# Two transposes swapped on a queue: k of batch b+1 ahead of C's exponentials of batch b, and the next loads placed behind q's transpose

## The chip, the cores and the metric

One core of one Trainium2 chip runs the whole kernel. The metric is the device time of one execution in microseconds (us); less is better. On one core, "slow" marks a run over 1.5% above the fastest of its kernel. Medians and ranges are over all executions, slow ones included. Ratios are the mean time of one kernel's fast runs over that of the other's fast runs of the same rounds, so they are not quite the ratio of the medians quoted beside them.

## The reference

Nystrom attention with 8 batches, 8 heads, 576 positions and 32 landmarks, followed by a gated feed-forward layer:

```python
q_lm = q.reshape(B, H, m, S // m, D).mean(axis=3)      # landmarks, k_lm likewise
A, Bm, C = sm(q, k_lm), sm(q_lm, k_lm), sm(q_lm, k)    # softmaxes
Z = Bm^T / (norms of Bm);  6 times: Z = 2 Z - Z @ Bm @ Z
x = A @ Z @ C @ v                                      # attention
out = (sigmoid(x @ w_gate) * (x @ w_val)) @ w_out
```

## The kernel before

The program is woven from streams (front, mid, value, norm, newton, ffn1, ffn2). A planning clock inside the kernel (`model`) guesses when each engine is free and when each tile has landed, and emits TensorE's instructions in the order of these guesses. On the chip that order is fixed: TensorE takes its instructions in turn, whatever is ready.

Names that the profiles use: klm and bq are the landmarks of k and q as TensorE takes them; bs, sl and sa are the scores of Bm, C and A; cl holds C's exponentials, ct the same transposed, cv is C @ v. Bc is Bm, Bt the same transposed; bdT and bd are Bt and Bc spread over the diagonal blocks of a larger matrix; s and sy belong to the iteration for Z. an is A. U and V are the rest of x times w_gate and w_val. gp and vp are the gate and value products of the feed-forward layer, th and ht what ScalarE and VectorE make of them, op the last product and ob its copy out of PSUM, where the kernel's matmuls leave their results. A transfer "lands" when its data has arrived.

The front of a late batch turns k and q by crossbar transposes issued on SP, sums them on GpSimd (POOL) to landmarks, and swaps halves by DMA:

```python
for what in ("k", "q") if b >= TURN else ():
    ...
    turned[what] = turn(t, ..., n, ...)                 # nc.sync.dma_start_transpose
for what in ("k", "q"):
    ...
    pool.tensor_add(out=s1, in0=t[:, :, 0:P6], in1=t[:, :, P6:2 * P6])    # 128 x 768
    pool.tensor_add(out=s2, in0=s1, in1=t[:, :, 2 * P6:3 * P6])           # 128 x 768
    if b >= SWAP and what == "k" and b < B - 1:
        load(b + 1, "k")
        load(b + 1, "q")
    ...                                                 # s3, s4: 128 x 256
# swaps of s4's halves by DMA on SP, then klm, bq on POOL, then load(b + 1, "v")
def fronts():
    for b in range(B):
        ...
        if b > TURN:
            yield made(turned_c, b - 1)                 # ct of b - 1 is issued
        yield from front(b)
```

The middle of a batch, on VectorE (DVE) between matmuls:

```python
turn(ct, ct, cl, ...)                                   # ct: C's exponentials, transposed
spread(bdT, Bt)          # two tensor_mul, blk x Bt, bf16, 128 x 128
...
dve.tensor_reduce(out=ce, in_=n1, axis=AX.X, op=ALU.max)            # n1 in PSUM (this is cc)
dve.tensor_scalar_add(out=ce, in0=cc, scalar1=1e-6)                 # 128 x 2, fp32
dve.reciprocal(out=rc, in_=ce)
...                      # S0 scaled by rc
spread(bd, Bc)           # two tensor_mul, blk x Bc, bf16, 128 x 128
```

The softmax here doesn't subtract the row's maximum and nothing guards it: scores larger than these inputs give would overflow.

Of the kernel before, what the change touches and what calls it, by code (L numbers as in the profile page):

```python
# [177 lines left out]
def kernel(ctx, tc, q, k, v, moe_w_gate, moe_w_val, moe_w_out, out):  # L178
# [14 lines left out]
    B, H, S, D = q.shape  # L193
# [20 lines left out]
    TURN, LATE = 3, 2  # L214
    PLAIN = min(TURN, LATE)

    SWAP = 3
# [14 lines left out]
    def bank(shape, dtype, name, hold=False):  # L232

        return model.take(ps.tile(shape, dtype, name=name, tag="p", bufs=BANKS), hold)

    def done_with(*tiles):
        model.held -= {t.name for t in tiles}

    def mm(slow=0.0, **kw):
        rhs, lhsT = kw["rhs"], kw["lhsT"]  # L240
        n = 1
        for x in rhs.shape[1:]:
            n *= x
        c = 1
        for x in lhsT.shape[1:]:
            c *= x
        nc.tensor.matmul(**kw)  # L247
        at = [x.start_partition() if hasattr(x, "start_partition") else 0 for x in (lhsT, kw["out"])]
        return model.pe(kw["out"], [lhsT, rhs], lhsT.shape[0], c, n, tuple(at), slow)
# [13 lines left out]
    def load(b, what, parts=1):  # L263
        src = {"q": q, "k": k, "v": v}[what]
        n = H // parts
        for x in range(parts):
            hs = slice(x * n, x * n + n)
            if x == 0:
                t = sb.tile([P6, H, NC * D], BF16, name=f"{what}n_{b}", tag=f"{what}n", bufs=2)
            nc.gpsimd.dma_start(  # L270
                out=t[:, hs], in_=src[b, hs].rearrange("h (p c) d -> p h (c d)", p=P6))
            landed = model.load(t, n * S * D * 2e-6, model.free["pe"])
            nat.setdefault((what, b), (t, []))[1].append(landed)
# [80 lines left out]
    square_of, turned_c, q_of = {}, {}, {}  # L354

    def copy(out, in_):

        if model.free["act"] + 0.1 < model.free["dve"]:
            return act.copy(out=out, in_=in_)
        return dve.tensor_copy(out=out, in_=in_)  # L360
# [26 lines left out]
    def front(b):  # L387

        bq = bq_p[b % 3]
        klm = sb.tile([128, H, m], BF16, name=f"klm_{b}", tag="klm", bufs=3)  # L390
        tT, turned, hls = {}, {}, {}

        def sums(what, n, hs, landed):

            k = hs.stop - hs.start
            if hs.start == 0:
                ends[what] = sb.tile([P6, H, 2 * D], BF16, name=f"ends_{b}{what}", tag="s1" if what == "k" else "s2", bufs=1)
            e = ends[what]
            model.waits[e.name] = landed
            copy(e[:, hs, 0:D], n[:, hs, (NC - 1) * D:])  # L400
            at = copy(e[:, hs, D:], n[:, hs, 0:D])
            lm = bank([128, k, m], FP32, f"lm_{b}{what}{hs.start}", True)
            for x in range(NC):
                for h in range(k):
                    mm(out=lm[:, h, :], rhs=seg3, start=(x + h == 0), stop=(x == NC - 1 and h == k - 1),
                       lhsT=n[:, hs.start + h, x * D:(x + 2) * D] if x < NC - 1 else e[:, hs.start + h])
            put(what, klm[:, hs], bq[:, hs], lm, b == 0)
            done_with(lm)

        ends = {}  # L410
        for what in ("k", "q") if b >= TURN else ():
            yield made(nat, (what, b))
            n, landed = nat.pop((what, b))
            t = sb.tile([128, H, HF], BF16, name=f"{what}T_{b}", tag=f"{what}T", bufs=2)
            tT[what] = t
            model.by_part.add(t.name)
            yield need(landed[-1])
            turned[what] = turn(
                t, t.rearrange("p h (c x) -> p (h c) x", c=3), n, n.rearrange("p h d -> p (h d)"))
        for what in ("k", "q"):  # L420
            if b >= TURN:
                t, done = tT[what], turned[what]
            else:
                n, landed = nat.pop((what, b))
                t = sb.tile([128, H, HF], BF16, name=f"{what}T_{b}", tag=f"{what}T", bufs=2)
                tT[what] = t
                model.by_part.add(t.name)
            for i in range(NP if b < TURN else 0):
                if b < LATE and i * len(landed) % NP == 0:
                    part = i * len(landed) // NP  # L430
                    yield need(landed[part], banks=1)
                    sums(what, n, slice(2 * i, 2 * i + H // len(landed)), landed[part])
                    if what == "q" and part == len(landed) - 1:
                        front_of[b] = (tT["q"], tT["k"], klm, bq)
                        lm_of[b] = ()
                yield need(landed[i * len(landed) // NP], banks=1)
                tp = bank([128, 2, HF], BF16, f"tp_{b}_{what}{i}")
                for h in range(2):
                    for c in range(3):
                        tr(  # L440
                            out=tp[:, h, c * P6:(c + 1) * P6],
                            in_=n[:, 2 * i + h, c * 128:(c + 1) * 128],
                            identity=ident[0:P6, 0:P6] if what == "k" or b >= PLAIN else
                            perm.rearrange("p r l -> p (r l)"),
                        )
                done = copy(t[:, 2 * i:2 * i + 2, :], tp)
            if b < LATE:
                continue

            s1 = sb.tile([128, H, P6], FP32, name=f"s1_{b}{what}", tag="s1", bufs=1)  # L450
            model.waits[s1.name] = done
            pool.tensor_add(out=s1, in0=t[:, :, 0:P6], in1=t[:, :, P6:2 * P6])
            s2 = sb.tile([128, H, P6], FP32, name=f"s2_{b}{what}", tag="s2", bufs=1)
            pool.tensor_add(out=s2, in0=s1, in1=t[:, :, 2 * P6:3 * P6])

            if b >= SWAP and what == "k" and b < B - 1:
                load(b + 1, "k")
                load(b + 1, "q")
            y = s2.rearrange("p h (l r) -> p h l r", r=3)
            s3 = sb.tile([128, H, m], FP32, name=f"s3_{b}{what}", tag="s3", bufs=1)  # L460
            pool.tensor_add(out=s3, in0=y[:, :, :, 0], in1=y[:, :, :, 1])
            s4 = sb.tile([128, H, m], FP32, name=f"s4_{b}{what}", tag="s4", bufs=2)
            pool.tensor_add(out=s4, in0=s3, in1=y[:, :, :, 2])
            if b >= SWAP:
                hls[what] = s4
                continue
            hl = sb.tile([128, 2, H, m], BF16, name=f"hl_{b}{what}", tag="hl", bufs=2)
            pool.tensor_copy(out=hl[:, 0], in_=s4)
            pool.tensor_sub(out=hl[:, 1], in0=s4, in1=hl[:, 0])
            hls[what] = hl  # L470
        q_of[b] = ()
        front_of[b] = (tT["q"], tT["k"], klm, bq)
        if b >= SWAP:
            other = {}
            for what in ("k", "q"):
                s4 = hls[what]
                yield need(s4)
                other[what] = sb.tile([128, H, m], FP32, name=f"s5_{b}{what}", tag="s5", bufs=2)
                for c in range(2):
                    nc.sync.dma_start(out=other[what][64 * c:64 * c + 64], in_=s4[64 - 64 * c:128 - 64 * c])  # L480
                model.swap(s4, other[what])
            yield need(other["q"])
            pool.tensor_add(out=klm, in0=hls["k"], in1=other["k"])
            for c in range(2):
                r = slice(64 * c, 64 * c + 64)
                pool.tensor_add(
                    out=bq[r, :, m * c:m * c + m], in0=hls["q"][r], in1=other["q"][r])
            if b < B - 1:
                lm_of[b] = ()
                yield made(mid_of, b - 1)  # L490
                load(b + 1, "v")
        if b < LATE or b >= SWAP:
            lm_of[b] = ()
        else:
            sums_of[b] = hls
# [468 lines left out]
    def step(s):  # L964
        return lambda: step_at.get(s)

    def made(where, b):
        return lambda: 0.0 if b in where else None
# [23 lines left out]
    def fronts():  # L992
        for b in range(B):
            yield (lambda: 0.0) if b < 2 else step(0) if b == 2 else made(mid_of, b - 2)
            if b > TURN:
                yield made(turned_c, b - 1)
            yield from front(b)

# [147 lines left out]
```

## Time and profile before

| | before |
|---|---|
| median, range of 3 runs | 271.88 us, 271.79 to 272.63 |
| profiled span, granted clock | 269.7 us, 0.998 |
| TensorE busy | 260.1 us (96%) |
| ct, k, q issued on SP in batch 3/4 | 89.43, 91.39, 94.90 us |
| bs of batches 4 to 7 starts on TensorE | 117.00, 146.91, 177.03, 206.03 us |

A page row gives busy time, share and instruction count by engine; the strips show the busy tenths of 40 slices. A waits row reads "who waited, for whom: us in total, times, longest us". A timeline row reads "start, us taken, engine, line, operation, out<-in, shape, count", with the idle time before it and its releaser in brackets. SPq marks the issue of a DMA; its landing comes later. The lines are in the prediction. This is batch 3, first VectorE, then POOL's first sum of the next k:

```profile
91.61 0.36 DVE L153 TENSOR_TENSOR bdT<-blk,Bt 128x128 bf16<-128x128 bf16 x2
93.60 0.17 DVE L153 TENSOR_SCALAR ce<-cc 128x2 f32<-128x2 f32 x1
94.60 0.35 DVE L153 TENSOR_TENSOR bd<-blk,Bc 128x128 bf16<-128x128 bf16 x2
```
```profile
98.36 1.64 POOL L153 TENSOR_TENSOR s_4k<-kT 128x768 f32<-128x768 bf16 x1 [12.90 <-DMA kT<-kn]
```

VectorE's three steps are over at 94.95 us; POOL's sums start 3.4 us later. The long POOL wait, which the change sets out to shorten, keeps the two apart.

### The profile page before, as it was taken

What the parts mean: (1) busy time and instruction counts of PE and PEld (TensorE: products, weight loads), DVE (VectorE), ACT (ScalarE), POOL (GpSimd) and SP (SyncE); (2) the same over time, 40 slices, a digit from 0 to 9 for tenths busy, and PEclk for the clock granted to TensorE, in tenths of its full rate; (3) what the DMA queues carried; (4) which work ended last, traced back from release to release, by engine and by line L of the source; (5) the groups of instructions that cost most, each with busy time, mean ns of one, the idle gap of its engine ahead of it and who ended that gap; (6) DMA issues with size and microseconds to landing.
All of it is one profiled execution on the core that took longest, in us unless ns stands there. A gap on an engine that the chain in (4) does not pass through costs nothing.

```text
span 269.7 us, 8019 instructions
## 1 busy us (share of the span) xinstructions
PE 260.1 (96%) x3089; PEld 167.0 (62%) x3123; DVE 193.3 (72%) x551; ACT 159.4 (59%) x413; POOL 96.2 (36%) x107
## 2 busy tenths in 40 slices
PE   8999999999999999999999999999999999999994
PEld 5877777757664666556646665556636664665443
DVE  4566888976899788948986778848968786963111
ACT  3663876866647754876477655875368643964001
POOL 8523231960874039511953078212922000000000
PEclk9999999999999999999999999999999999999999
DMA  6999999999795998889794989589530413101433
GB/s 94 193 206 205 205 206 206 205 203 172 141 194 115 204 170 121 181 135 199 141 221 72 182 157 203 129 139 199 124 90 12 97 41 80 41 0 41 117 103 92
DMA packets 62645, 38.00 MB, mean 141 GB/s; under 512 B 33552, under 2 KB 58128, under 8 KB 62608
## 3 DMA queue, kind: packets, MB, share of 16 engines
q0 software_dynamic: 23600, 18.88, 47.0%
q1 hardware_dynamic: 38896, 18.52, 31.4%
q8 instruction: 24, 0.39, 0.6%
q14 instruction: 13, 0.11, 0.1%
q10 hardware_dynamic: 112, 0.10, 0.1%
HBM read 37.75 MB, written 9.44 MB: 175 GB/s over the span
## 4 chain that ended last, share of the span: by engine, by line
PE 93%; ACT 2%; issue 2%; POOL 1%; DVE 0%; POOLq 0%; ACTq 0%
PE op L247 34%; PE gp L247 18%; PE vp L247 18%; PE idle_ps L247 3%; PE pn L247 2%; PE cv L247 2%; PE rb L247 2%; PE sc L247 1%; PE sa L247 1%; PE tp_q L252 1%; PE up_1g L247 1%; PE up_0g L247 1%; PE up_2g L247 1%; PE tp_k L252 1%; PE up_1v L247 1%
## 5 line engine op out<-in xcount | busy, mean ns | idle before, releaser
L247 PE MATMUL op<-wo_sb,ht 128*128 128x512 bf16 (+1 forms) x410 | 109.4, 373 | 2.1 <-issue 1.1
L153 ACT ACTIVATE th<-gp 128x288 bf16<-128x288 f32 x192 | 76.7, 415 | 48.4 <-PE gp L247 36.7
L153 DVE SCALAR_TENSOR_TENSOR ht<-th,vp 128x288 bf16<-128x288 bf16 x192 | 82.0, 448 | 21.9 <-ACT th L153 17.2
L247 PE MATMUL gp<-an,U 128*128 128x288 bf16 x384 | 78.5, 286 | 0.3
L247 PE MATMUL vp<-an,V 128*128 128x288 bf16 x384 | 78.4, 286 | 0.0
L247 PEld LDWEIGHTS <-ht 128*128 128x128 bf16 x444 | 39.9, 98 | 26.7 <-issue 5.8
L247 PEld LDWEIGHTS <-U 128*128 128x128 bf16 x384 | 35.9, 98 | 27.3 <-issue 2.5
L247 PEld LDWEIGHTS <-V 128*128 128x128 bf16 x384 | 37.5, 98 | 9.7 <-issue 0.2
L153 ACT ACTIVATE ob<-op 128x512 f32<-128x512 f32 (+1 forms) x31 | 18.2, 587 | 29.6 <-PE op L247 24.2
L153 DVE SCALAR_TENSOR_TENSOR sy<-sy,pn 128x384 bf16<-128x384 bf16 x35 | 19.2, 548 | 2.3 <-PE pn L247 1.9
L153 DVE TENSOR_SCALAR ob<-op 128x512 f32<-128x512 f32 (+2 forms) x7 | 4.2, 596 | 17.3 <-PE op L247 17.3
L247 PE MATMUL idle_ps<-idle_w 128*128 128x256 bf16 x86 | 14.8, 308 | 1.2 <-DVE idle_w L297 1.2
L247 PE MATMUL pn<-sy 128*128 128x192 bf16 (+1 forms) x84 | 13.1, 237 | 0.4 <-ACT kT L153 0.3
L153 DVE TENSOR_TENSOR an<-aexp,rb 128x384 bf16<-128x384 bf16 (+1 forms) x32 | 12.4, 446 | 0.3 <-PE rb L247 0.3
L247 PEld LDWEIGHTS <-sy 128*128 128x128 bf16 x88 | 8.1, 97 | 6.2 <-DVE sy L153 2.8
L153 ACT ACTIVATE aexp<-sa 128x288 bf16<-128x288 f32 x32 | 10.7, 418 | 1.5 <-PE sa L247 1.1
L247 PEld LDWEIGHTS <-idle_w 128*128 128x128 bf16 x86 | 8.5, 109 | 3.3 <-DVE idle_w L297 1.2
L247 PEld LDWEIGHTS <-WT 64*32 64x32 bf16 x384 | 3.8, 89 | 9.1 <-issue 6.6
L270 POOL DMA_DIRECT2D kn<-in_k_dram x9 | 7.0, 779 | 4.6 <-DMA wg_sb<-in_moe_w_gate_dram 2.1
L153 DVE CAST U<-up_0g 128x512 bf16<-128x512 f32 x8 | 5.5, 690 | 4.1 <-PE up_0g L247 4.1
L270 POOL DMA_DIRECT2D vn<-in_v_dram x8 | 6.3, 789 | 5.3 <-PE gp L247 4.5
L270 POOL DMA_DIRECT2D qn<-in_q_dram x9 | 6.8, 753 | 4.0 <-PE sm L247 2.2
(201 smaller groups left out, 349.7 us busy)
## 6 DMA issues: line engine op xcount, KB each, us to landing
vn<-in_v_dram POOLq DMA_DIRECT2D x8, 576.0 KB, 9.4
kn<-in_k_dram POOLq DMA_DIRECT2D x7, 576.0 KB, 8.1
qn<-in_q_dram POOLq DMA_DIRECT2D x7, 576.0 KB, 10.6
out_dram<-ob SPq DMA_DIRECT2D x53, 64.0 KB, 3.0
out_dram<-ob SPq DMA_DIRECT2D x17, 192.0 KB, 2.3
out_dram<-ob SPq DMA_DIRECT2D x18, 128.0 KB, 2.4
wg_sb<-in_moe_w_gate_dram POOLq DMA_DIRECT2D x3, 512.0 KB, 19.7
wv_sb<-in_moe_w_val_dram POOLq DMA_DIRECT2D x3, 512.0 KB, 21.0
```

What stands on the lines that cost most here:

```text
L153: f(**kw)
L247: nc.tensor.matmul(**kw)
L252: nc.tensor.transpose(**kw)
L270: nc.gpsimd.dma_start(out=t[:, hs], in_=src[b, hs].rearrange("h (p c) d -> p h (c d)", p=P6))
```

## The change

Intent: k's transpose and sums need nothing of batch b, so let them go ahead of ct of b and shorten the loop. Loads follow q's transpose, to leave it the DMA engines. The diff, cut to its core:

```diff
-        for what in ("k", "q") if b >= TURN else ():
+        def turned_by_dma(what):
             ...
+        for what in ("k", "q") if TURN <= b <= SWAP else ():
+            yield from turned_by_dma(what)
         for what in ("k", "q"):
+            if b > SWAP:
+                if what == "q":
+                    yield made(turned_c, b - 1)
+                yield from turned_by_dma(what)
+                if what == "q" and b < B - 1:
+                    load(b + 1, "k")
             ...
-            if b >= SWAP and what == "k" and b < B - 1:
+            if b == SWAP and what == "k":
                 load(b + 1, "k")
+                load(b + 1, "q")
+            elif b > SWAP and what == "q" and b < B - 1:
                 load(b + 1, "q")
 ...
-            if b > TURN:
+            if TURN < b <= SWAP:
                 yield made(turned_c, b - 1)
```

TURN and SWAP are both 3, so batches 4 to 7 are concerned.

## The prediction

> **What bounds the kernel now.** I read the page first: busy shares, the strip of 40 slices, the chain that ended last.
>
> ```profile
> PE 260.1 (96%) x3089; PEld 167.0 (62%) x3123; DVE 193.3 (72%) x551; ACT 159.4 (59%) x413; POOL 96.2 (36%) x107
> ...
> PE   8999999999999999999999999999999999999994
> ...
> POOL 8523231960874039511953078212922000000000
> PEclk9999999999999999999999999999999999999999
> DMA  6999999999795998889794989589530413101433
> ...
> PE 93%; ACT 2%; issue 2%; POOL 1%; DVE 0%; POOLq 0%; ACTq 0%
> ```
>
> TensorE is busy in every slice after the first, at a granted clock of 0.998, and carries 93% of the chain that ended last. POOL and the DMA have holes, so what the change touches isn't what fills the span. Next I cut the span into 10 us windows. From 56 to 256 us PE is busy 197.5 of 200 us; from 256 to 269.7 us, 9.8 of 13.7. So of 9.6 us without PE work, some 2.7 lie in the first 30 us, 3.9 in the last output's eviction and store, and only about 2.5 us in the middle, where the change acts. Most of that is a small gap on each return from packed small matmuls to full ones (0.16 us "issue").
>
> Then I asked for the waits. PE's own list holds nothing from a crossbar transpose; POOL's does:
>
> ```profile
> PE op L247 <- issue: 1.1, 7, 0.2
> ...
> PE pn L247 <- ACT kT L153: 0.3, 1, 0.3
> ```
> ```profile
> POOL s_4k L153 <- DMA kT<-kn: 12.9, 1, 12.9
> POOL s_6k L153 <- DMA kT<-kn: 11.5, 1, 11.5
> POOL s_5k L153 <- DMA kT<-kn: 11.3, 1, 11.3
> POOL s_7k L153 <- DMA kT<-kn: 10.4, 1, 10.4
> ```
>
> POOL idles 10 to 13 us per late batch for k's transpose, and PE does not notice. The timeline of SP (the queue that issues transposes and stores) shows why POOL waits: k's transpose stands behind that of C's exponentials (ct), which needs the previous batch's scores.
>
> ```profile
> 89.43 1.85 SPq L384 DMA_TRANSPOSE ct<-cl  x1
> 91.39 3.40 SPq L384 DMA_TRANSPOSE kT<-kn  x1
> 94.90 3.60 SPq L384 DMA_TRANSPOSE qT<-qn  x1
> 98.59 6.98 SPq L959 DMA_DIRECT2D out_dram<-ob  x8
> 105.67 1.11 SPq L480 DMA_DIRECT2D s_4k<-s_4k  x2
> ```
>
> There is a serial loop: ct of batch b, kT and qT of b+1, POOL's sums, swaps of halves by DMA, bq, scores, ct of b+1. It turns in about 30 us (bs of batches 4 to 7 starts at 117.00, 146.91, 177.03, 206.03). PE's work per batch is about as long, and bq is ready 1.5 to 2.6 us before bs asks for it (for batch 4: 114.81 against 117.00). The loop is nearly, not actually, the bound.
>
> **What the Trainium skill says.** "Perfetto Trace Analysis", section "Identifying the Most-Contended Engine": matmul busy share is no measure of the distance to roofline, because matmuls are pipelined. That warns me not to call 96% optimal. But the change alters no matmul, so what matters is idle time, and there is little. The same page, "DMA Instruction — HWDGE (DVE, Sync)": the reported window ends at the issue, data movement lies outside. The trace agrees: the median kT window is 3.9 us, its landing 5.9 us after issue; I use landings. "DMA: Bandwidth & Descriptors", section "Issuing engines are not separate DMA queues": all DMAs end on the same 16 engines and interleave. POOL's loads and SP's transposes can therefore slow each other; no run here measures that yet. Its section "Silent corruption: two transposing streams in flight at once" doesn't bite: every transpose stays on SP.
>
> **The change part by part.** The comparison of instruction order shows equal totals: the same 3,123 matmuls by kind and shape, 82 DMAs on SP, equal POOL work; one output eviction goes from DVE to ACT. So nothing is removed or added, only moved:
>
> - kT of b+1 goes ahead of ct of b (for batch 4 right behind the store of tile 3, about 83.9 instead of 91.39 us: 7.5 us sooner).
> - POOL's four k sums (1.64 + 1.65 + 1.52, some 4.9 us with gaps) then run while ct and qT are under way. In before, the k sums, two load issues (1.56) and q sums stood in a row.
> - k's next load is issued after q's transpose is, q's next load after q's first sums; before, both stood behind k's first sums.
> - The kernel plans its emission with timings of its own, so PE's order follows. I walked both PE orders with start-to-start durations from the timeline (op 0.2155 us, gp and vp 0.1225, a packed score 0.024 to 0.036, pn 0.083, 0.15 on return to full matmuls). The walk puts before's bs of batch 7 at 207.1 (trace 206.03). Bs of batches 4 to 7 comes earlier by 2.8, 5.5, 8.3 and 14.5 us, but the last gp and last op stay at the same place: ffn2 matmuls fill what is vacated. Sum before 267.17, after 267.02: 0.15 us gained, since returns from packed work fall from 30 to 29. **That is the whole direct gain.**
>
> What could be lost: does the data keep up with the earlier positions? I chain the after queue by hand with measured times (store issue 0.4 to 0.5 us per DMA, kT landing 5.9, qT 5.6, swap issue to bq complete 3.5 to 6). With each bound store at its shifted eviction:
> - Batch 4: kT lands 89.8, sums to 94.7; qT lands 96.9, sums to 102.6; the q swap waits for tile 6's store (103.4 to 105.2); bq at 108.8. PE asks at 114.3: margin 5.5.
> - Batches 5 and 6: bq about 136 and 162.6, asked for at 141.5 and 168.7: margin 5 to 6.
> - Batch 7: the q swap stands behind tile 18's store, evicted about 186.2; swap at 187.0, bq at 190.6 with the short swap (3.6, as in batch 7 before, when loads were over). PE asks at about 191.5: margin 1, or 1.5 short with a 6 us swap.
> - ct of batch 4: its scores come 2.8 us sooner, but on SP the four stores of tile 8 stand ahead (117.5 to 119.2). It issues at 119.3, as before (119.13), lands 4.6 later at 123.9; cv is now asked for at 123.4 instead of about 126. Short by 0.5 us.
>
> So I expect perhaps 0.5 us of new PE wait at batch 4 and 0.3 on average at batch 7: +0.8, against -0.15 from the order. There are 2.5 us of gaps at most to win in the middle, mostly not of this kind.
>
> **Rivals.** (1) *Breaking the loop is a real gain.* For it: POOL's 10 to 13 us waits and the 30 us loop. Against it: PE doesn't wait for it and the tail after 246 us is 8 output tiles of pure op matmuls in both. At most 2 us: 270. (2) *PE's order now runs ahead of the data.* For it: the plan takes no time for stores on SP's queue, yet SP issues in order and stores block swaps and ct (s_7q ended POOL's 5.2 us wait in before). PE follows its own fixed order, so one late tile stops it. Against it: the margins above grow in three of four batches. If one wait of 1.5 us occurs per batch: 277. (3) *Transfers collide.* kT now overlaps the load of v; loads of k and q are apart, each with more of the engines. If kT took 8 us instead of 5.9, margins of 5 would hold; batch 7 is bound by the store, not kT. Within 0.5 us of no effect. (4) *ACT or DVE becomes the bound* because 12 us of batch 7's small work bunches sooner: DVE is at 72%, ACT at 59%, no instruction is added; a few tenths.
>
> **Range and chances.** 271.88 - 0.15 + 0.8 gives 272.5; part of the doubtful waits may be spread away, as each estimate of a start has an error of about 1 us, so I say **272.3 us**. Low end: no wait and half a microsecond of gaps gained, 271.0. High end: waits of 1 to 1.5 us in two places, 274.2. Faster by 2% (below 266.4) would need over 5 us, more than all idle time of the middle: 1%. Slower by 2% (above 277.3) needs rival 2 in nearly every batch: 4%. Within 2%: 95%.
>
> **What would show it right or wrong.** Right: PE busy stays near 260 us; POOL's waits for kT shrink; kT is issued before ct; bs of batch 7 starts near 192; the last op matmul ends where it did (about 266). The waits list would show PE or its weight loads waiting for ct of batch 4 or bq of batch 7, each under 1.5 us. Wrong: PE waits of several us behind bq, ct or sl, kT landings well over 8 us, or a busy sum of PE that falls, which would mean the spacing of matmuls depends on what they are interleaved with.

## The result, and the profile after

The changed kernel took 276.19 us in the median of 4 runs (274.59 to 279.66, of which the last is slow) against 271.95 us in the same rounds: ratio 1.0131, 95% interval 1.0082 to 1.0181. Repeated in 6 runs it gave 277.5 us (273.81 to 280.2; the four fast ones reach 277.62), ratio 1.0155 (1.0103 to 1.0207). It is slower by 1.3 to 1.6%, outside the predicted range, and its executions spread more than those of the kernel before. The profiled execution is a fast one with a span of 273.8 us, 4.1 us longer. Page lines after:

```profile
PE 264.5 (97%) x3123; PEld 168.1 (61%) x3123; DVE 196.3 (72%) x550; ACT 159.0 (58%) x414; POOL 95.9 (35%) x107
...
PEclk9999999999999999999999999999999999999999
...
PE 84%; DVE 5%; DMA 5%; ACT 3%; issue 1%; POOL 1%; DVEq 0%; ACTq 0%; POOLq 0%
```

The clock is not the cause of this profile's loss: 1.0. (PE's busy sum isn't comparable to a few us: the profile before lacks 34 of 3,123 matmuls.) The chain that ended last tells: PE's share fell from 93 to 84%, and DVE and DMA, at or near zero before, hold 5% each. POOL's waits did shrink, for batch 4 from 12.9 to 9.0 us:

```profile
POOL s_4k L153 <- DMA kT<-kn: 9.0, 1, 9.0
...
POOL s_6k L153 <- DMA kT<-kn: 8.5, 1, 8.5
```

The queue view (SP) of the same place as in the prediction. k's transpose is ahead at 84.71 us instead of 91.39, but its issue holds the queue 5.57 us, a store's four DMAs follow, and ct comes at 92.40 instead of 89.43:

```profile
84.71 5.57 SPq L384 DMA_TRANSPOSE kT<-kn  x1
90.38 1.93 SPq L972 DMA_DIRECT2D out_dram<-ob  x4
92.40 1.50 SPq L384 DMA_TRANSPOSE ct<-cl  x1
94.01 3.22 SPq L384 DMA_TRANSPOSE qT<-qn  x1
```

k's transposes also land later after their issue. From the tile view of kT, before and then after:

```profile
DMA to landing us min/median/max: 5.4/5.9/6.8
```
```profile
DMA to landing us min/median/max: 5.6/8.5/10.2
```

Now batch 3's middle after the change: VectorE, POOL, and TensorE in turn.

```profile
94.71 0.92 DVE L153 TENSOR_SCALAR ce<-cc 128x2 f32<-128x2 f32 x1
95.94 0.61 DVE L153 TENSOR_SCALAR sy<-s,rc 128x128 bf16<-128x128 f32 x2
96.46 1.08 DVE L153 TENSOR_TENSOR bd<-blk,Bc 128x128 bf16<-128x128 bf16 x2
```
```profile
93.97 1.64 POOL L153 TENSOR_TENSOR s_4k<-kT 128x768 f32<-128x768 bf16 x1 [8.98 <-DMA kT<-kn]
95.68 1.64 POOL L153 TENSOR_TENSOR s_4k<-s_4k,kT 128x768 f32<-128x768 f32 x1
```
```profile
96.60 0.40 PE L247 MATMUL vp<-an,V 128*128 128x288 bf16 x2 [0.45 <-DVE sy L153]
97.95 0.41 PE L247 MATMUL gp<-an,U 128*128 128x288 bf16 x2 [0.52 <-DVE ht L153]
```

An addition on two elements per partition, 0.17 us before, takes 0.92 us and ends at 95.63, right after POOL's first sum (95.61). bd's pair takes 1.08 instead of 0.35 us; its first half ends after POOL's second sum (97.32). sy, whose input is in PSUM, takes 0.61 us as ever. The Trainium skill, "SBUF — State Buffer", section "SBUF: two separate sides", says why: GpSimd and VectorE share a pair of SBUF ports as "an **exclusive lock**, not a bandwidth split", which a VectorE instruction needs when it runs in a 2-port mode, or when it reads two SBUF tensors while the GpSimd instruction reads SBUF as well. The trace agrees: ce reads fp32 from SBUF (no trace shows which mode it ran in), bdT and bd read two SBUF tensors, and of VectorE's instructions that overlap POOL's sums these three alone are ever slow. The gates ht, with one input in PSUM, have a mean of 447 ns where they overlap POOL's arithmetic and 449 ns elsewhere (74 and 118 instances, before).

Aligning both traces matmul by matmul, and each with its own order walked as in the prediction, shows where the 4.1 us went: 1.13 at batch 2, 1.3 at batch 3, about 1.5 at batch 4 (all with PE waiting for VectorE), 0.4 at batch 5 (for ct). Batch 2 is chance, not the change: both programs are the same there. k's transpose of batch 3 landed 0.33 us earlier, so POOL's sum began at 67.94, before ce (68.12), not after it (68.27 against 68.13); the repeat's profile does not have this stall.

### The profile page after: what moved, and what is told of

It reads as the page before. It is cut to its first block, busy times and chain, and to the rows that moved or that the text cites. A ratio compares the mean times of both kernels' runs of the same rounds, so it can differ in the third digit from the quotient of the medians.

```text
span 273.8 us, 8037 instructions
## 1 busy us (share of the span) xinstructions
PE 264.5 (97%) x3123; PEld 168.1 (61%) x3123; DVE 196.3 (72%) x550; ACT 159.0 (58%) x414; POOL 95.9 (35%) x107
## 4 chain that ended last, share of the span: by engine, by line
PE 84%; DVE 5%; DMA 5%; ACT 3%; issue 1%; POOL 1%; DVEq 0%; ACTq 0%; POOLq 0%
PE op L247 31%; PE gp L247 16%; PE vp L247 15%; DMA ct<-cl 2%; DMA qn<-in_q_dram 2%; PE pn L247 2%; PE idle_ps L247 2%; DVE ht L153 2%; PE cv L247 2%; PE rb L247 2%; DVE ce L153 1%; PE up_0g L247 1%; PE sc L247 1%; PE up_2g L247 1%; PE up_1g L247 1%
## 5 line engine op out<-in xcount | busy, mean ns | idle before, releaser
L247 PE MATMUL op<-wo_sb,ht 128*128 128x512 bf16 (+1 forms) x444 | 116.8, 374 | 0.1
L153 ACT ACTIVATE ob<-op 128x512 f32<-128x512 f32 (+1 forms) x32 | 18.8, 588 | 27.1 <-PE op L247 24.5
L153 DVE TENSOR_SCALAR ob<-op 128x512 f32<-128x512 f32 (+2 forms) x6 | 3.5, 580 | 16.7 <-PE op L247 16.7
L247 PE MATMUL idle_ps<-idle_w 128*128 128x256 bf16 x86 | 14.2, 299 | 1.2 <-DVE idle_w L297 1.2
L153 ACT ACTIVATE cl<-sl 128x288 bf16<-128x288 f32 x20 | 8.0, 418 | 0.1
## 6 DMA issues: line engine op xcount, KB each, us to landing
qn<-in_q_dram POOLq DMA_DIRECT2D x7, 576.0 KB, 10.2
```

Of the source, the lines that this page charges most:

```text
L153: f(**kw)
L247: nc.tensor.matmul(**kw)
```

## The experiments

After this reading I had two theories. **Port conflict**: the earlier sums of k meet bdT, ce and bd, VectorE falls behind, PSUM banks come free late, PE stalls. **Order ahead of the data**: PE's fixed order asks for ct and bq before they land, because the planning clock doesn't know of the stores on the queue and of the longer landings. Rivals: the moved loads, and the transfers' collision. Fifteen kernels ran. "Held" and "free" below tell whether POOL's sums were kept off VectorE's instructions.

| run | median us | ratio to before (95%) |
|---|---|---|
| change, repeated | 277.5 | 1.0155 (1.0103–1.0207) |
| ce removed, bd early | 278.95 | 1.0177 (1.0129–1.0224) |
| same edits, kernel before | 272.39 | 1.0020 (0.9994–1.0047) |
| before, POOL kept busy | 274.54 | 1.0121 (1.0081–1.0161) |
| order only | 274.99 | 1.0124 (1.0062–1.0186) |
| loads only | 272.68 | 1.0038 (0.9991–1.0085) |
| change without v's loads | 277.4 | 1.0191 (1.0136–1.0246) |
| same, ce removed, bd early | 280.51 | 1.0325 (1.0252–1.0398) |
| change, held | 275.9 | 1.0143 (1.0098–1.0188) |
| corrected clock: change, free | 278.41 | 1.0239 (1.0192–1.0286) |
| corrected clock: change, held | 274.11 | 1.0090 (1.0060–1.0119) |
| corrected clock: before | 274.15 | 1.0084 (1.0060–1.0108) |
| later swap: change, held | 273.12 | 1.0039 (1.0011–1.0067) |
| later swap: change, free | 275.22 | 1.0092 (1.0047–1.0138) |
| later swap: before | 272.06 | 1.0004 (0.9973–1.0036) |

### First set: is it the port conflict?

The change, unedited, again:

> The changed kernel unaltered, for a firm ratio and for its spread. All theories: 274.5 to 277 us in the fast state. The lock theory (a VectorE instruction that needs the port pair shared with GpSimd waits until the GpSimd instruction in progress ends) adds: in the profile ce (mean ns of a free one 169) takes about 0.9 to 1.5 us in batches 3 and 4, and bd 0.8 to 0.9 us; batch 2 has it in some executions only, since k's transpose there lands within 0.2 us of ce.

Its profile has bd at 944 ns (batch 3), 1234 ns (4), ce 1323 and bd 785 ns (5), bd 835 ns (6). So bd was met as expected, but ce of batches 3 and 4 was not (195 and 169 ns): which instruction is met differs between executions of one program. It also has PE waiting 1.1 us for ct at batch 5.

ce and bd taken out of the way, TensorE's order kept but for 7 small matmuls:

```diff
-        mm(out=n1, lhsT=blk, rhs=Bc, start=True, stop=(b > 0))
+        mm(out=n1, lhsT=blk, rhs=Bc, start=True, stop=False)
+        ... nc.tensor.matmul(out=n1, lhsT=eps, rhs=idle_w[:, 0:2 * m], start=False, stop=True)
-            dve.tensor_scalar_add(out=ce, in0=cc, scalar1=1e-6)
         spread(bdT, Bt)
+        for g in range(2):                              # bd here, no longer behind S0
+            nc.vector.tensor_mul(out=bd[:, g], in0=blk, in1=...)
```

> The changed kernel, PE, ACT, GpSimd and queue order untouched, with the two VectorE instructions that met GpSimd's sums taken out of their way: ce's 1e-6 is summed by a TensorE matmul (as batch 0 has it), bd is made right after bdT, before the sums start. Lock theory: the stalls at batches 2, 3 and 4 (1.1, 1.3 and 1.5 us) go, so about 272 us (271.5 to 273). Rival (stores ahead of ct and bq on the queue, or the new matmul order itself): unchanged, 275 to 276.5 us.

It missed: 278.95 us (277.0 in its three fast runs), no better than the change. Its profiled execution was a slow one (clock 0.986), but up to 146 us its granted clock was 1.0, and its PE waits name what came instead:

```profile
PE cv L247 <- DMA ct<-cl: 2.6, 2, 1.5
PE vp L247 <- DVE ht L153: 1.6, 1, 1.6
PE bs L247 <- POOL bq L153: 1.6, 1, 1.6
```

With VectorE quick again at batches 3 and 4, PE reaches cv earlier and stands there for ct, 1.11 us at batch 3 and 1.47 us at batch 4. In the change itself VectorE's delay covered such a wait at batch 4: ct landed at 126.68 us, cv began at 127.13, and 1.4 us of the stalls lie just before it. At batch 3 it did not: ct had landed at 96.36 us, cv began at 99.05, and 1.3 us of stalls lie between. And at batch 6 the conflict had only moved: bdT took 1.4 and the early bd 1.7 us. So at batch 4 one cause hid behind the other, and this edit removed neither cleanly.

The same edits in the kernel before:

> Control: the same two edits in the kernel before, where the sums start 3 to 4 us after ce and bd in batches 3 to 7. Lock theory: 271.5 to 272.2, at most 0.5 us gained (batch 2's bd waited 0.65 us). If the edits help by themselves, the kernel before gains as much as the changed one (about 4 us), and the lock theory falls.

272.39 us, ratio 1.0020: no gain, as expected. The edits are worth nothing by themselves.

The kernel before, POOL kept busy where it idles:

```diff
+        if b >= SWAP:
+            for _ in range(6):
+                nc.gpsimd.tensor_add(out=scr, in0=scr, in1=scr)   # scratch, nobody waits
```

> The kernel before with its own order, and six adds of 128 x 768 on a scratch tile (about 10 us) that nobody waits for, in the time in which GpSimd is idle in batches 3 to 7, so that it is busy when bdT, ce and bd are made. No transfer and no other engine's order changes. Lock theory: bdT, ce and bd wait up to 1.6 us each, PE loses 1.3 to 4 us in each of 5 batches: 278 to 290 us. Rivals: GpSimd has slack there, so 271.5 to 272.5 us.

274.54 us, ratio 1.0121. The direction holds and rules out "POOL has slack, so its place is free": POOL's adds (9.2 us) end before kT lands, so that its own sums start at 98.37 us instead of 98.36, and yet the kernel lost 3.0 us (1.2%).

```profile
91.77 1.35 DVE L153 TENSOR_TENSOR bdT<-blk,Bt 128x128 bf16<-128x128 bf16 x2
```
```profile
85.27 9.18 POOL L496 TENSOR_TENSOR scr<-scr 128x768 bf16<-128x768 bf16 x6
```

bdT's first half took 1.2 us at batch 3 instead of 0.22. The matmuls of the two profiled runs are the same in the same order. Aligned, the one with adds falls behind by 0.84, 0.45, 0.33 and 0.40 us at batches 3 to 6, each time at the matmuls that need bdT or at sa: 2.0 of the 2.1 us between the spans. The size was less than expected: the adds met one to three of the three instructions per batch, most of them near the add's end (waits of 0.1 to 1.0 us), and PE absorbed a part.

### Second set: which half, and the transfers

Only the order of the transposes, loads as before:

> The first half of the change alone: k's transpose and sums of batch b+1 ahead of ct of b; the loads of k and q stay where the kernel before has them. If the new place of k's transpose does the harm (it holds the queue ahead of ct while v's load is in flight, and its sums meet ce and bd), 274 to 278 us, as the whole change. If the moved loads do the harm, 271.5 to 272.5.

274.99 us, ratio 1.0124: nearly the whole loss is in this half.

Only the loads moved, order ct, k, q:

> The second half alone: order of transposes as before (ct, k, q), next k load behind k's sums, next q load behind q's first sums. ct stands first on the queue and GpSimd's sums come after ce and bd, so both theories of the harm (ct late, shared port) say 271.3 to 272.5 us; 274 or more if the loads' place is the cause.

272.68 us, ratio 1.0038 with an interval that includes 1. No instruction of VectorE from batch 3 on is slow in its profile, and ct is first on the queue.

Without v's loads in batches 4 to 7 (wrong results; every engine's order kept):

```diff
+            if what == "v" and b > SWAP:       # batch 3's v is used again; the clock is told as before
+                landed = model.load(v3[0], ...)
+                continue
```

> The changed kernel with its order on every engine, but v of batches 4 to 7 is not loaded (batch 3's v is used again; wrong results on purpose). The transfer-collision theory: k's transpose, no longer beside v's load, is issued in 3.4 us instead of up to 5.6 and lands in 6 us instead of 8.5 in the median; cv no longer waits for ct (1.1 to 1.4 us in the profile of the repeat and of the run without port conflicts); what is left are VectorE's waits for GpSimd: 272 to 274.5 us. If v's load doesn't matter, 275 to 278 as the changed kernel.

The mechanism held and the time missed. kT's issue took 3.88 us at batch 4 (5.57 in the change), landing fell to 5.6 us in the median, ct landed 3.7 to 3.9 us after its issue (up to 6.8 in the change, 8.7 in the repeat), and PE's waits for ct vanished; so the collision with v's load is real. But it took 277.4 us: as kT landed earlier, the sums started earlier and met bdT as well (967, 719, 1407 and 1283 ns in batches 3 to 6). Of the longer span in this profile some 1.6 us were lost before 60 us: PE waited 1.7 us for batch 0's k at the start, and the granted clock then was 0.67 (8 to 10 us) and 0.50 (10 to 12 us). No edit touches that.

The same with ce removed and bd early:

> As the run without v's loads, and with ce and bd out of GpSimd's way. If the two causes together are the whole loss: 271.2 to 272.5 us, no PE wait over 0.6 us after 90 us. If it stays at 274 or more, a third cause exists (stores ahead of bq or ct on the queue, or the order of matmuls).

280.51 us, the slowest (its four runs had clocks of 0.992 to 0.998). The label promises too much: bd now stood where the earlier sums are. VectorE's timeline of batch 3, then PE's waits:

```profile
92.90 0.57 DVE L153 TENSOR_TENSOR bdT<-blk,Bt 128x128 bf16<-128x128 bf16 x2
93.40 1.79 DVE L644 TENSOR_TENSOR bd<-blk,Bc 128x128 bf16<-128x128 bf16 x2
```
```profile
PE vp L247 <- DVE ht L153: 4.4, 3, 1.6
```

This answers for the second miss, too: the conflict must be removed by time, not by moving its victims.

### Third set: held sums, corrected clock

POOL reads one element of bd before it sums, so it cannot start earlier. Both transposes are emitted before the sums; the queue keeps the order k, ct, q:

```diff
+            yield made(bd_of, b - 1)
+            pool.tensor_copy(out=seen, in_=bd_of[b - 1][:, 1, 3, 31:32])
             pool.tensor_add(out=s1, ...)
```

> The change, but GpSimd's sums of k of batch b+1 first read one element of bd of batch b, so they cannot start before bdT, ce and bd are done: the port conflict is gone for good, not moved as in the earlier attempt; k's transpose still goes ahead of ct. bdT, ce, bd then take 0.17 to 0.23 us each in all batches from 3 on. If the conflict were the whole loss: 271.3 to 272.5 us. With late ct and bq as a second cause: 273 to 276, with PE waits for ct or bq of 0.5 to 1.5 us each.

275.9 us. In its profile, a fast run of 274.23 us, no VectorE instruction is slow from batch 3 on, and one stall is left, at batch 7:

```profile
197.85 0.22 PE L247 MATMUL bs<-klm,bq 64*32 64x32 bf16 x8 [1.75 <-POOL bq L153]
198.65 0.31 PE L247 MATMUL sl<-kT,bq 64*32 64x288 bf16 x7 [0.45 <-POOL bq L153]
```

The prediction saw a shortage at this place, and q's swap does stand behind a store (192.18 us, swap at 193.41). But the changed kernel itself has no such wait: there the store came at 190.14 us, bq was ready at 194.57 and bs asked for it at 195.51. The edit moved some matmuls in the planned order, so the size of this wait belongs to the held kernel. The two waits are 2.2 of the 2.5 us by which the profiled run is longer than before's. The other three executions took 275.7 to 277.0 us at a clock of 0.994, against 1.0 in the profiled one; what else they lost no profile shows.

The planning clock corrected, sums free:

```diff
-        end = self.free["sp"] + (3.0 if self.free["dma"] > start else 2.5)
+        end = self.free["sp"] + (5.0 if self.free["dma"] > start else 2.5)
                 (nc.scalar if x and r else nc.sync).dma_start(out=dst[:, cs], in_=ob[r:r + n, :])
+                model.free["sp"] = max(model.free["sp"], model.landed[_handle(ob)]) + 0.45
```

> The change with the kernel's own planning clock corrected, so that TensorE's order asks for ct and bq later: each store takes 0.45 us of the queue, and a transpose beside other transfers lands 5.0 us (not 3.0) after its issue. Nothing else differs. If TensorE's order running ahead of the data is the main loss: 271.5 to 273 us, no PE wait for ct or bq over 0.3 us; VectorE's waits for GpSimd may stay, up to 1.5 us. If the port conflict is the main loss: 274 to 277.

Corrected clock and held sums:

> Both: corrected planning clock and sums that wait for bd. If the two causes are the whole loss: 271.2 to 272.6 us, neither faster nor slower than before, and no PE wait over 0.5 us after 90 us. Over 274: a third cause.

Corrected clock, kernel before:

> Control: the kernel before with the corrected planning clock. TensorE bounds it either way and nothing waited: 271.0 to 272.6 us. If it gains over 1 us, the planning clock is worth more than the change by itself.

278.41, 274.11 and 274.15 us. The corrected clock costs the kernel before 2.5 us (ratio 1.0084), so all three levels I had named are off by that much; its order starts batch 3's bs at 89.94 instead of 83.97 us, and why this costs so much I did not pursue. Against this control the three settle the port conflict: PE waits for neither ct nor bq in any of them; free sums cost 4.3 us, held ones nothing. Free and held kernel have the same 3,123 matmuls in the same order, so nothing of TensorE's plan differs between them; aligned, the free one falls behind at batches 4, 5 and 6, at the matmuls that need bdT, at gp, vp and at sa, by 4.4 us in all. VectorE, batch 4, free and then held:

```profile
124.50 1.81 DVE L153 TENSOR_TENSOR bdT<-blk,Bt 128x128 bf16<-128x128 bf16 x2
127.21 0.76 DVE L153 TENSOR_SCALAR ce<-cc 128x2 f32<-128x2 f32 x1
128.81 0.95 DVE L153 TENSOR_TENSOR bd<-blk,Bc 128x128 bf16<-128x128 bf16 x2
```
```profile
125.04 0.36 DVE L153 TENSOR_TENSOR bdT<-blk,Bt 128x128 bf16<-128x128 bf16 x2
126.30 0.17 DVE L153 TENSOR_SCALAR ce<-cc 128x2 f32<-128x2 f32 x1
127.30 0.35 DVE L153 TENSOR_TENSOR bd<-blk,Bc 128x128 bf16<-128x128 bf16 x2
```

### Fourth set: both causes, with the kernel's own clock but one number

To settle it without the 2.5 us, only the swap's landing in the planning clock was put 2 us later:

```diff
-        end = max(self.free["sp"], self.free["dma"]) + 2.5
+        end = max(self.free["sp"], self.free["dma"]) + 4.5
```

Change, held:

> The change, its sums held until bd is made, and the planning clock told that a swap of halves lands 2 us later (4.5 instead of 2.5), which is what bq of batch 7 was short of (1.75 and 0.45 us) in the run with held sums; nothing else of the planning clock altered. Two-cause theory: no PE wait over 0.5 us after 90 us; 271.3 to 272.8 us, level with the kernel before. Third cause: 274 or more.

Change, free:

> The change with the later swap in the planning clock alone; sums free to meet bdT, ce and bd. Two-cause theory: the port conflict is back, 1 to 2 us of VectorE time in two to four batches, PE waits for VectorE (ht, bdT) of 2 to 5 us in sum: 274 to 277 us, at least 1.5 us over the run with held sums.

Kernel before:

> Control: the kernel before with the later swap in its planning clock: 271.3 to 272.8 us, as before, and equal to the run with held sums within 1 us.

273.12, 275.22 and 272.06 us. The control is level with before. The free sums cost 2.1 us more than the held ones (1.6 between the means of fast runs, and one free run took 272.70); PE waits for bdT again. This pair is weaker than the last: its matmul orders differ, and the two intervals overlap. The held kernel is 1.1 us above the control, and its profile has one large wait left, which the expectation had excluded:

```profile
190.42 0.56 PE L247 MATMUL cv<-vn,ct 96*32 96x64 bf16 x48 [1.23 <-DMA ct<-cl]
```

So with the conflict gone and bq in time, what is left is one wait for ct, 1.23 us. The two theories together account for most of the loss in the profiled runs. Not all: this run's span is 2.0 us longer than its control's (271.15 and 269.13), in another matmul order, so 0.8 us stay unexplained, and a smaller third cause isn't excluded. No version beat the kernel before; its median is the lowest throughout.

## Why the prediction was wrong

- **The bound and the ceiling** were right: TensorE's work is the same, no kernel went below 271.5 us in the median, and shortening POOL's waits gained nothing.
- **The step that failed** is the second part of "part by part": POOL's k sums "then run while ct and qT are under way", counted as free. They run in the very 4 us in which VectorE makes ce and bd. Rival 4 asked about VectorE's busy share and "no instruction is added; a few tenths". The share was never the question; the same instructions got longer. In the profiled run ce and bd take 5.9 us more than free ones, batch 2 included. With ct and bq out of the picture the conflict costs 4.3 us (corrected clock, same matmul order) or 2.1 us (later swap, orders that differ).
- **The late data: mechanism right for ct, size wrong.** The prediction expected 0.5 us of wait for ct of batch 4 and 0.3 for bq of batch 7. In the changed kernel's profiles PE waited for ct at batch 5: 0.4 us, and 1.1 in the repeat. With VectorE's delay out of the way (batches 3 and 4 of the slow profile) it waited 1.11 and 1.47 us for ct of batches 3 and 4. The mis-sized term is the landing of kT, 5.9 us in the chain of sums: beside v's load it was 8.4 to 10.2 us at batches 4 to 7, one of the prediction's own signs of being wrong, and the issue held the queue 5.57 us at batch 4. The margins of bq at batches 4 to 6, 5 to 6 us in the prediction, were 1.4, 1.8 and 1.6 us (for batch 4, bq was ready at 115.38 us and bs started at 116.79). For batch 7 the margin of 1 us was right: 0.9. A wait for bq showed only in edited kernels (1.75 and 0.45 us with held sums).
- **Rival 3** (transfers collide) was dismissed by looking at kT's own margin. The collision was there; its harm went through ct, which was issued later, behind kT and a store, at batch 3 (92.40 us) and landed later at batch 5 (6.8 us after its issue, 8.7 in the repeat; 3.8 to 5.1 in the kernel before).
- **Terms were added that are not additive.** A wait for VectorE ahead of cv covers a wait for ct, as at batch 4 of the change. That is one reason why no removal alone gained anything (278.95, 277.4, and 275.9 us with held sums). The other is that the first two edits brought other instructions of VectorE under the sums.
- The prediction's count of 82 DMAs on SP is not that of the traces, which list 126 in both kernels. That the totals are equal holds.
- Open: the spread of the changed kernel's executions (273.8 to 280.2 us) is not settled. The three longest have lower clocks (0.986 to 0.991), but the fast ones at 0.998 to 1.0 still spread by 3.8 us. Batch 2's conflict, decided by 0.1 to 0.3 us of a transfer's landing, shows one way in which it can arise.

## What to carry to other kernels

Idle time of an engine off the critical path can be what keeps it out of another's way: before moving work into it, list what the engine that shares its ports does at that moment, instruction by instruction, not by share of the span. On an in-order queue, charge a moved transfer to everything behind it, and with the issue time that it has beside the other transfers in flight there. When removing one suspected cause gains nothing, look in the trace for the wait that took its place before dropping the theory.

## What the Trainium skill lacked or had wrong

- "SBUF — State Buffer", "SBUF: two separate sides", had the decisive rule right, and I had not applied it. It gives no measured case of a small VectorE instruction that waits: ce, 2 elements per partition, 0.17 us when free, took up to 1.51 us behind one GpSimd add of 1.64 us (the change); bdT up to 1.67 instead of 0.22 us (corrected clock, free).
- "Perfetto Trace Analysis", "DVE / Act Engine Instruction", starts VectorE's reported window at execution and doesn't say where a wait for the shared ports shows. Here it lies inside the window and counts as busy: ce of 1.48 us at batch 2 has no gap of that size before it.
- "DMA: Bandwidth & Descriptors", "DMA Transpose (X-bar)", has no figure for a transpose beside a load: at batch 4 the issue held the queue 5.57 us against 3.88 us without v's load, and the median landing over five transposes was 8.5 against 5.6 us.
